# A new order of steps in the ramp and the first quarter of stage 1, in a one-core adaLN, linear attention and gMLP kernel

## The chip, the core and the metric

The kernel runs on one core of a Trainium2 chip. A core has a matrix engine (PE, with its own row PEld for the loading of weights), a vector engine (DVE), an activation engine (ACT), a general engine (POOL) and a queue engine (SP) that here issues most DMAs. Each engine works through its own list of instructions strictly in order and waits at an instruction until its inputs are there and its output buffer is free. The metric is the device time of one execution in microseconds (us).

## What is computed

```
def _A_ref(x, wqkv, w_phi, wo):
    q, k, v = qkv[0], qkv[1], qkv[2]              # of x @ wqkv, 16 heads of 28
    pq = einsum('bhsd,hdf->bhsf', q, w_phi); pk = einsum('bhsd,hdf->bhsf', k, w_phi)
    phi_q = concat([softmax(pq), softmax(-pq)]); phi_k = concat([softmax(pk), softmax(-pk)])
    kv = einsum('bhsf,bhsd->bhfd', phi_k, v); z = sum over s of phi_k
    o = (phi_q @ kv) / (phi_q . z + 1e-6)
    return o @ wo
def _B_ref(x, w_in, w_sp, b_sp, w_out):
    z = gelu(x @ w_in); z1 = z[..., :Fh]; z2 = layernorm(z[..., Fh:])
    g = einsum('ts,bsf->btf', w_sp, z2) + b_sp
    return (z1 * g) @ w_out
mod = silu(c) @ w_mod                              # sa, ca, ga, sb, cb, gb
x = x + ga * _A_ref(layernorm(x) * (1 + ca) + sa, ...)
x = x + gb * _B_ref(layernorm(x) * (1 + cb) + sb, ...)
```

x is 2048 rows of 448, all in bf16; Fh is 896.

## The kernel before

The fast path is written as one long list of words, the table ORDER. Each word is a step; a small loop at the end of `fast_path` runs the words from first to last and so emits the instructions. Since every engine keeps the order in which its instructions were emitted, the table sets the order on each engine and on each DMA queue, and nothing else does. A word reads name:arguments, then `@slot` for a PSUM buffer (A0, A1, A2 of two banks, B0, B1 of one) and `/V`, `/S`, `/G`, `/Y` for the engine that does it (DVE, ACT, POOL, SP). A slot is free again when the step that reads the last result out of it is done.

The 2048 rows are 16 tiles of 128. The steps that matter here:

- `ld:` loads: x0 to x5 are parts of x, wq, wk and wv the three parts of wqkv, phi is w_phi, wsa and wca the shift and scale columns of w_mod for the first half, wsb and wcb for the second, wmga and wmgb the gates.
- Ramp. `FTk`, `FTq` (L795) transpose the key and query weights on PE, 8 transposes a step, `ETk`, `ETq` copy them out (L799 on ACT, L801 on DVE), `bd` (L739) spreads phi into a block-diagonal BD, `PFk`, `PFq` (L811, 4 matmuls) multiply, so that phi is folded into the weights Wk and Wq; `EPk`, `EPq` copy out. `csA`, `ccA` (L747, 16 small matmuls) give shift and scale columns, `esA` and `ecA` copy them (ecA gives the gain column f_ca, L751). `SHk`, `SHq`, `SHv` (L761) work out a shift row, `SCk`, `SCq`, `SCv` (L770 on ACT, L772 on POOL, L774 on DVE) scale the weights by the gain, step 0 out of PSUM, steps 1 to 3 in SBUF. `du` (L712) multiplies zeros, as filler on PE.
- Layer norm of tile i: `l1s` (L818, L819: statistics, on DVE), `l1e`, `l1r` (L822, L823, L826: on POOL for one to four tiles), `l1a` (L829: normalise, on DVE or POOL). Tiles 0 to 3 are turned on PE (`X`, L842) and copied (`XE`), the others by DMA transposes on SP (`T1`, L834).
- Stage 1, per tile: `kM`, `vM` (L852, L860: 4 matmuls), `kE`, `kF` (L855: the two exponentials, on ACT), `vC` (L863: copy, on ACT), `kS` (L866: sums, on DVE), `kR` (L870: reciprocal, on DVE, into one of two buffers), `kP` (L873: f_phik, the normalised features, on DVE or POOL, in a ring of four), `kA` (L883: 8 matmuls that add to kvacc in slot A0). `qM` (L907) and `qE`, `qF` (L912) make query features; `gr`, `ge` (L918, L921) a gate row, `wos`, `wts` (L924) multiply output weights by it. `W:0,u` (L1051) are transposing loads of w_sp on SP.

Stage 2 (`nM` and on) forms the attention output, the second layer norm and the first matmuls of the second half; stage 3 (`gM`, `oM`) mixes over rows and writes out.

Of the kernel before, what the change touches and what calls it, by code (L numbers as in the profile page):

```python
# [486 lines left out]
SHk@B0 XE:3/S XE:2/S ld:wv/Y ld:x3/Y SCk:0/S ld:x4/Y SHv@B1 SCk:2/V SCk:1/V SCv:2/V SCv:3/V l1s:4 l1s:5 l1s:6 l1s:7 l1s:8 l1s:9 l1s:10 ld:wmgb/Y
ld:x5/Y ld:wo/Y ld:wmga/Y SCv:1/S SCv:0/S l1e:4,8/G l1r:4,8 l1a:5/G l1a:4/G SCk:3/S qM:0@A2 vM:0@B0 qF:0 vC:0 qE:0 kM:0@B1 vM:1@A1 vC:1 kE:0 kM:1@B0
vM:2@A2 vM:3@A1 l1a:6/G l1a:7/G kF:0 kF:1 kE:1 vC:2 kM:2@B1 kM:3@B0 kS:0 l1s:11 kS:1 kR:0 l1e:8,12/G l1r:8,12 kP:0/V kR:1 kP:1/G l1a:9/G vC:3 kE:2
qM:1@A2 gr:1@A1 kF:3 kE:3 kF:2 ge:1 qE:1 T1:4,6 kA:0@A0 gr:0@B0 kM:4@B1 qF:1 kF:4 kE:4 kS:2 kS:3 kR:2 l1s:12 T1:6,8 ld:wout/Y qM:2@A1 kA:1@A0 kM:5@B1  # L490
kR:3 kP:2/V l1a:8/G kP:3/G kS:4 l1s:13 kR:4 kP:4/V T1:8,10 W:0,2 W:0,5 l1a:10/G wts:4/G l1a:11/G T1:10,12 ge:0 ld:wsb/S qF:2 kA:2@A0 vM:4@B0 kA:3@A0
kE:5 kF:5 kM:6@B1 l1s:14 l1s:15 l1e:12,16/G l1r:12,16 l1a:13/G vC:4 qE:2 kE:6 kF:6 kA:4@A0 vM:5@B0 kM:7@A2 kM:8@B1 vM:6@A1 kE:7 vC:5 kF:7 kS:5 kR:5
l1a:15/G l1a:14/G kP:5/V kS:6 kS:7 kR:6 kR:7 kP:6/V kP:7/V l1a:12/G T1:12,14 wos:0/G kF:8 T1:14,16 ld:win1/Y W:0,0 W:0,1 ld:wcb/Y W:0,7 ld:bsp/Y W:0,4
vC:6 kA:5@A0 vM:7@B0 kM:9@A2 vM:8@A1 kE:8 kF:9 vC:7 kE:9 kA:6@A0 kM:10@B1 kE:10 kF:10 vC:8 kA:7@A0 kM:11@B0 vM:9@A2 kM:12@B1 kF:11 kE:11 W:0,3
ld:win0/Y vC:9 kS:8 kR:8 kS:9 kR:9 kP:8/G kS:10 kS:11 kR:10 kP:9/G kR:11 kP:10/V kP:11/G kA:8@A0 kE:12 kF:12 vM:10@B0 kM:13@A2 vC:10 kA:9@A0 kF:13
kE:13 kS:12 kR:12 kP:12/G kS:13 kR:13 kP:13/G vM:11@B0 vC:11 kA:10@A0 kM:14@B1 kE:14 kF:14 wts:0/G wos:1/G wts:6/G wos:2/G wts:2/G wts:1/G wos:3/G
kA:11@A0 kS:14 kR:14 kP:14/V vM:12@B0 kM:15@A2 vC:12 kF:15 kE:15 vM:13@B1 vC:13 kA:12@A0 kS:15 kR:15 kP:15/V vM:14@B0 kA:13@A0 vM:15@B1 vC:14 vC:15
kA:14@A0 csB@B0 kA:15@A0 esB KV:0/V KV:1/V KZ:0 KZ:1 qM:3@A2 ccB@B0 nM:0@A1 nM:1@A0 ecB qF:3 nX:0 SHw:3@B0 SHw:2@B1 nX:1 nC:0 nC:1 nS:0 nT:0 nA:0/V
T2:0,1 W:0,6 nT:1 SCw:3,1/G SCw:1,1/G SCw:0,2/V SCw:0,3/V SCw:2,1/V nA:1/G T2:1,2 qE:3 qM:4@A2 qM:5@A1 qF:4 qE:4 nM:2@A0 nM:3@A2 nX:2 nC:2 nX:3 nC:3
nS:1 qF:5 nT:2 nT:3 qE:5 wN:0@B0 wR:0/S SHw:1@B1 nM:4@A1 nM:5@A0 SCw:0,1/S nX:4 nX:5 nC:4 nC:5 nS:2 nA:2/G nT:4 nA:3/G nT:5 nA:4/G wN:1@B0 wQ:0/S  # L500
wR:1/S wQ:1/S SHw:0@B1 SCw:2,0/S l2R:0,2/G l2r:0,2 l2a:0/G SCw:0,0/V nA:5/V T2:2,4 T2:4,6 qM:6@A2 nM:6@A1 nM:7@A0 wN:2@B0 wN:3@B1 qE:6 nX:6 nC:6 nX:7
nC:7 nS:3 nT:6 nT:7 qF:6 wR:2/S wQ:2/S wR:3/S wQ:3/V l2R:2,4/V nA:6/G nA:7/G l2r:2,4 l2a:3/G l2a:2/G qM:7@A2 nM:8@A1 nM:9@A0 wN:4@B0 wM:5@B1 W:1,1
# [12 lines left out]
zN:12/V zN:13/G zQ:14/V yM:3,6@B1 yM:0,3@A1 yM:1,6@B0 yG:0,3 yG:1,6 yM:1,0@A0 yG:1,0 yG:3,6 yM:3,3@A1 yM:0,5@B0 yG:0,5 yG:3,3 yG:0,6 zR:14,16/V
zW:14,16 zN:14/G zN:15/V gM:0,6@B1 gM:0,3@B0 gG:0,3 gM:0,4@A2 gG:0,6 gM:0,2@B0 yM:2,4@B1 yM:2,6@A1 yG:2,6 yG:2,4 gG:0,4 gG:0,2 yM:3,5@A2 yM:3,1@B0
yM:2,3@B1 yG:3,5 wts:5/V yG:2,3 yG:3,1 gM:0,0@A2 gG:0,0 gM:0,5@B0 gG:0,5 yM:2,0@B1 gM:0,1@A2 gG:0,1 gM:1,4@B0 oM:0,0,7@A2 oM:3,0,7@A1 yM:3,4@A0 gG:1,4
oE:0 oM:2,0,7@B0 yM:3,2@A2 yG:3,4 yG:2,0 yG:3,2 guard@A0 gM:1,5@B1 oM:1,0,7@A2 oE:1 oE:2 oE:3 gM:1,2@A0 gG:1,2 gM:1,1@B0 gM:1,3@A2 gM:1,0@A1 gG:1,3
gG:1,0 gM:1,6@A2 oD:0/Y oD:3/Y oD:2/Y gG:1,1 gG:1,5 gG:1,6 gM:2,0@B0 yM:2,2@B1 yG:2,2 W:3,0 W:3,3 W:3,7 W:3,1 W:3,6 W:3,4 W:3,2 gM:2,2@A2 gG:2,0
oM:6,0,7@B0 gM:2,3@B1 oM:4,0,7@A1 gM:2,5@A0 oE:4 gG:2,5 gG:2,3 gM:2,6@A1 gG:2,6 gG:2,2 oM:5,0,7@B1 oE:5 oE:6 gM:2,4@A0 gM:2,1@B0 gG:2,1 oM:7,0,7@B1  # L520
oE:7 W:3,5 oD:1/Y gM:3,3@A2 read gG:2,4 oM:8,0,7@B0 oE:8 oM:10,0,7@B1 oM:9,0,7@B0 oE:9 oE:10 oD:8/Y oD:10/Y oD:6/Y oD:5/Y gM:3,2@A1 gM:3,5@B0
gM:3,1@B1 gG:3,1 gG:3,2 gM:3,6@A0 gM:3,4@B1 gG:3,6 gG:3,4 gG:3,3 gG:3,5 oD:7/Y gM:3,0@A1 oM:11,0,7@B1 gM:4,2@B0 oD:4/Y gG:3,0 oM:12,0,7@A2 oE:11 oE:12
oM:13,0,7@B1 oE:13 gG:4,2 oD:9/Y gM:4,6@A2 gM:4,4@A1 gM:4,3@B0 gM:4,0@B1 gG:4,4 gG:4,3 gG:4,0 gM:4,1@A1 gM:4,5@B0 hint oM:14,0,7@B1 gG:4,1 gG:4,6
gG:4,5 oM:15,0,6@B0 oM:15,6,7@B0 oE:14 oE:15 oD:12/Y oD:13/Y oD:14/Y oD:11/Y oD:15/Y
"""


def fast_path(tc, A_x, A_wqkv, A_w_phi, A_wo, B_w_in, B_w_sp, B_b_sp, B_w_out, c, w_mod, out, flag):
    nc = tc.nc
    S = A_x.shape[1]  # L530
# [82 lines left out]
    scb = aph.tile([DC, KC, P], BF, name="f_scb")  # L613
# [92 lines left out]
            for h in range(2):  # L706
                nc.tensor.matmul(wps[:, h, 0:256], lhsT=zero[64 * h:64 * h + 64, 0:P], rhs=zero[64 * h:64 * h + 64, 0:256], start=True, stop=True)

    def du(n, slot):
        wps = bank(slot, "warm_ps")  # L710
        for _ in range(n):
            nc.tensor.matmul(wps[:, 0, 0:256], lhsT=zero[:, 0:P], rhs=zero[:, 0:256], start=True, stop=True)  # L712
# [465 lines left out]
```

## Time and profile before

| what | us |
|---|---|
| median of 3 runs | 262.6 (262.52 to 263.1) |
| the profiled execution, its own time | 262.55 |
| its span, first instruction to last | 260.8 |
| PE, DVE, ACT, POOL busy | 251.9, 159.1, 107.6, 89.1 |

The span is what the trace shows; the rest of the execution's own time lies around it. In the rows of the timeline the columns are the start (us from the span's start), the time to the end of the last of the instructions that a row merges, engine, line, operation, output and inputs, and in brackets how long the engine stood idle before it and what released it. Matmuls are pipelined: a matmul's row is longer than the step from one matmul's start to the next, so starts are compared with starts.

### The profile page before, as it was taken

How to read it: one execution, taken by the hardware profiler on the slowest of the kernel's cores; microseconds unless marked ns; L12 is line 12 of the kernel's file. 1: busy time of each engine (PE TensorE's matmuls, PEld its weight loads, DVE VectorE, ACT ScalarE, POOL GpSimd, SP SyncE). 2: the span in 40 equal slices, each digit the busy share in tenths (PEclk: the TensorE clock that was granted, in tenths of full speed). 3: DMA queues.
4: the chain of work that ended last, by engine and by line, in shares of the span. 5: the costliest groups of instructions: out<-in, count | busy, mean ns of one | idle time of the engine just before them, and what ended most of it. 6: DMA issues, size and time to landing. Idle time of an engine off the chain costs nothing.

```text
span 260.8 us, 4339 instructions
## 1 busy us (share of the span) xinstructions
PE 251.9 (97%) x1636; PEld 134.8 (52%) x1636; DVE 159.1 (61%) x359; ACT 107.6 (41%) x222; POOL 89.1 (34%) x149
## 2 busy tenths in 40 slices
...
GB/s 170 282 302 124 211 132 224 234 219 64 57 112 134 86 145 114 184 130 176 139 0 3 1 0 0 20 3 75 0 3 161 141 0 0 20 106 0 3 38 62
DMA packets 68655, 25.23 MB, mean 97 GB/s; under 512 B 58129, under 2 KB 68498, under 8 KB 68626
## 3 DMA queue, kind: packets, MB, share of 16 engines
...
q8 instruction: 15, 0.25, 0.4%
q14 instruction: 14, 0.11, 0.1%
...
## 4 chain that ended last, share of the span: by engine, by line
PE 81%; DVE 12%; DMA 2%; ACT 1%; issue 1%; POOL 1%; SPq 0%; ACTq 0%; DVEq 0%
PE g_ps L1059 37%; PE z_ps L1043 9%; PE z_ps L1015 9%; PE o_ps L1072 8%; DVE f_t L955 3%; PE v_ps L860 3%; PE x_ps L971 3%; PE k_ps L852 3%; PE kvacc L883 2%; PE q_ps L907 2%; DMA f_wk_raw<-in_A_wqkv_dram 2%; DVE f_ksum L866 2%; PE num L935 1%; DVE f_phik L873 1%; PE sh_ps L761 1%
## 5 line engine op out<-in xcount | busy, mean ns | idle before, releaser
L1059 PEld LDWEIGHTS <-f_z2n 128*128 128x128 bf16 x560 | 50.1, 98 | 47.0
L1065 DVE TENSOR_TENSOR f_gb<-g_ps,f_bsp 128x512 f32<-128x512 f32 (+2 forms) x35 | 20.4, 583 | 55.8 <-PE g_ps L1059 55.7
L1059 PE MATMUL g_ps<-f_Eq,f_z2n 128*128 128x512 bf16 x224 | 49.5, 379 | 0.0
L1046 ACT ACTIVATE f_z1T<-z_ps 128x512 bf16<-128x512 f32 x28 | 15.6, 592 | 61.8 <-PE z_ps L1043 61.7
L1015 PE MATMUL z_ps<-f_win,f_hT 112*128 112x448 bf16 (+1 forms) x128 | 26.2, 352 | 0.0
L1043 PE MATMUL z_ps<-f_hT,f_win 113*128 113x512 bf16 (+1 forms) x112 | 26.1, 379 | 0.0
L1059 PE MATMUL g_ps<-f_hT,f_z2n 128*128 128x384 bf16 (+1 forms) x224 | 25.1, 272 | 0.0
L1059 PE MATMUL g_ps<-f_wsp,f_z2n 128*128 128x512 bf16 x112 | 24.7, 379 | 0.0
L1072 PE MATMUL o_ps<-f_wout,f_z1T 128*128 128x448 bf16 x112 | 23.0, 352 | 0.0
L1075 DVE TENSOR_TENSOR f_xpad<-o_ps,f_x 128x448 bf16<-128x448 f32 x16 | 9.6, 620 | 20.7 <-PE o_ps L1072 20.7
L1066 DVE TENSOR_TENSOR f_z1T<-f_gb,f_z1T 128x512 bf16<-128x512 f32 (+2 forms) x35 | 20.5, 585 | 1.5
L1015 PEld LDWEIGHTS <-f_hT 112*128 112x128 bf16 (+1 forms) x128 | 12.2, 97 | 12.4 <-DMA f_hT<-f_xpad 0.8
L912 ACT ACTIVATE f_Eq<-q_ps 112x1024 bf16<-112x1024 f32 x16 | 16.1, 1028 | 5.8 <-PE q_ps L907 5.8
L855 ACT ACTIVATE f_E<-k_ps 128x448 bf16<-128x448 f32 x32 | 15.9, 550 | 4.4 <-PE k_ps L852 2.5
L1043 PEld LDWEIGHTS <-f_win 113*128 113x128 bf16 (+1 forms) x112 | 10.9, 97 | 13.1 <-issue 0.2
L866 DVE TENSOR_REDUCE f_ksum<-f_E 128x32 f32<-128x896 bf16 x16 | 16.7, 1060 | 0.7 <-ACT f_E L855 0.7
L955 DVE TENSOR_TENSOR f_t<-num,f_w 128x896 bf16<-128x896 f32 x16 | 16.8, 1084 | 0.4
L1019 ACT ACTIVATE f_z2g<-z_ps 128x896 bf16<-128x896 f32 x16 | 14.7, 917 | 4.0 <-PE z_ps L1015 3.6
L1072 PEld LDWEIGHTS <-f_z1T 128*128 128x128 bf16 x112 | 10.9, 98 | 10.1
L907 PE MATMUL q_ps<-f_hT,f_Wq 113*128 113x512 bf16 (+1 forms) x64 | 15.2, 379 | 0.6 <-DVE f_t L955 0.6
L860 PE MATMUL v_ps<-f_wv,f_hT 113*128 113x448 bf16 (+1 forms) x64 | 14.6, 352 | 0.0
L852 PE MATMUL k_ps<-f_Wk,f_hT 113*128 113x448 bf16 (+1 forms) x64 | 14.4, 352 | 0.0
...
## 6 DMA issues: line engine op xcount, KB each, us to landing
...
```

Source lines behind the costliest of these rows:

```text
L852: nc.tensor.matmul(t[:, 0, 0:D], lhsT=hT[0:KR[m], i, m, :], rhs=Wk[0:KR[m], m, :], start=(m == 0), stop=(m == KC - 1))
L860: nc.tensor.matmul(t[:, 0, 0:D], lhsT=hT[0:KR[m], i, m, :], rhs=wv[0:KR[m], m, :], start=(m == 0), stop=(m == KC - 1))
L866: nc.vector.tensor_reduce(out=ksum[:, i], in_=Er[i % NR][:].rearrange("p s (c f h) -> p (s c) h f", c=4, h=HP), axis=AX.X, op=ALU.add)
L907: nc.tensor.matmul(t[:, u, :], lhsT=Wq[0:KR[m], m, cc * CB:cc * CB + P], rhs=hT[0:KR[m], 4 * st:4 * st + 4, m, :], start=(m == 0), stop=(m ...
L912: nc.scalar.activation(out=Eq[st // 2][0:CB, 2 * c2:2 * c2 + 2, s, (st % 2) * 512:(st % 2 + 1) * 512], in_=ps["q" + str(n)][0:CB, :, :], f ...
L955: nc.vector.tensor_tensor(out=tr[i % 2][:], in0=numv(i)[:, :, :, 0:DH], in1=wr[i // 2 % 2][:, i % 2].unsqueeze(3).to_broadcast([P, 2, H, D ...
L1015: nc.tensor.matmul(t[:, hf, 0:D], lhsT=hT[0:KR[m], i, m, :], rhs=win_s[0:KR[m], m, FH + hf * D:FH + (hf + 1) * D], start=(m == 0), stop=(m ...
L1043: nc.tensor.matmul(t[:, 0, :], lhsT=win_s[0:KR[m], m, fc * P:(fc + 1) * P], rhs=hT[0:KR[m], 4 * st:4 * st + 4, m, :], start=(m == 0), stop ...
L1059: nc.tensor.matmul(g[:, 0, 0:b - a], lhsT=later["z2n"][:, s_, fc * P:(fc + 1) * P], rhs=wspT[t][:, s_, a:b], start=(s_ == 0), stop=(s_ == ...
L1065: nc.vector.tensor_tensor(out=gb, in0=ps["G%d_%d" % (ch, fc)][:, 0, 0:b - a], in1=bsp[:, t * TCHF + a:t * TCHF + b], op=ALU.add)
L1066: nc.vector.tensor_tensor(out=z, in0=gb, in1=z, op=ALU.mult)
L1072: nc.tensor.matmul(ps["o" + str(t)][:, 0, 0:D], lhsT=later["z1T"][:, fc, t * P:(t + 1) * P], rhs=wout_s[:, fc, :], start=(fc == 0), stop=( ...
```

## The change

The words of ORDER up to `vC:6` (tile 6 of stage 1) are put in another order; behind it the words stay in their order and only some slots get other names. The set of steps is the same. Assignments to engines change too: BD goes from DVE to POOL, ETk:0, ETq:0, SCk:0, SCv:0, l1a:0, 4, 11 and 13, wts:4 and kP:3 to DVE, kP:5 and kP:7 and two SCv to POOL, and others between DVE and ACT. `du` takes a second argument that it does not use, and wsb is loaded from SP's queue instead of ACT's.

```diff
-m3 m4 m1/G m2b/V m2a/V ld:x0/Y ld:wq/Y l1s:0 ld:c/S du:3@A2 ct@B0 tbl ce:1 ce:2 l1e:0,1/G l1r:0,1 l1a:0/G ce:3 ce:4 du:11@A2 FTq:0@B1 du:1@A2 FTq:1@B0
-ETq:0/S X:0@A2 XE:0/S ld:wk/Y FTk:1@A1 ETk:1/S FTk:0@B1 ETk:0/S ld:phi/Y ETq:1/V bd/V scb ld:x1/Y l1s:1 l1e:1,2/G l1r:1,2 l1a:1/G PFq:3@B0 PFq:2@A2
...
+m3 m4 m1/G m2b/V m2a/V ld:x0/Y ld:wk/Y ld:phi/Y ld:c/S du:3,0@A2 ct@B0 tbl ce:1 ce:2 l1s:0 du:11,1@A2 FTk:1@B1 ld:wq/Y FTk:0@A0 ld:x1/Y du:1,4@A1
+du:4,3@A1 ETk:0/V bd/G ETk:1/S PFk:1@A1 ld:wsa/Y PFk:2@A2 PFk:0@B1 EPk:1/S FTq:0@A0 l1e:0,1/G ld:x2/Y FTq:1@A1 ld:wca/Y l1r:0,1 EPk:2/S EPk:0/S ce:3
...
-    def du(n, slot):
+    def du(n, k, slot):
```

SP's queue at the start, before and then as changed. f_wk_raw, f_wq_raw and f_wv are the key, query and value weights, f_wm the shift and scale columns:

```order
 L641 DMA f_x<-in_A_x_dram 128x448
-L630 DMA f_wq_raw<-in_A_wqkv_dram 112x4x448
 L630 DMA f_wk_raw<-in_A_wqkv_dram 112x4x448
 L634 DMA f_phi<-in_A_w_phi_dram 112x4x28
+L630 DMA f_wq_raw<-in_A_wqkv_dram 112x4x448
 L642 DMA f_x<-in_A_x_dram 128x448
+L637 DMA f_wm_123<-in_w_mod_dram 112x4x464
 L643 DMA f_x<-in_A_x_dram 128x2x448
```

The key weights and phi are now ahead of the query weights, and the first columns of w_mod ahead of rows 2 and 3 of x.

POOL's list in the first half of stage 1, where f_phik is kP, f_xpad is l1a and f_wo, f_wout are wos and wts. Before:

```order
L873 TENSOR_TENSOR f_phik<-f_E_128,f_kr_134 128x896
L829 TENSOR_SCALAR f_xpad<-f_x,f_nm_147,f_rs_146 128x4x112 x2
L873 TENSOR_TENSOR f_phik<-f_E_130,f_kr_134 128x896
L829 TENSOR_SCALAR f_xpad<-f_x,f_nm_147,f_rs_146 128x4x112
L924 TENSOR_TENSOR f_wout<-f_wout,f_g_rep 128x448
```

and now:

```order
L924 TENSOR_TENSOR f_wo<-f_wo,f_g_rep 112x448
L873 TENSOR_TENSOR f_phik<-f_E_128,f_kr_134 128x896
L822 TENSOR_SCALAR f_rs_146<-f_mv_145 128x4
L823 TENSOR_SCALAR f_nm_147<-f_mv_145 128x4
L826 TENSOR_TENSOR f_rs_146<-f_rs_146,f_mhalf 128x4
L829 TENSOR_SCALAR f_xpad<-f_x,f_nm_147,f_rs_146 128x4x112 x3
```

The gate row of f_wo (wos:0) now stands ahead of the first kP on POOL (kP:1), and the last three of POOL's tiles are normalised (f_rs, f_nm, f_xpad) between it and the next two, kP:5 and kP:7.

DVE's list from kS:4 to kP:6, as changed (f_kr_133 and f_kr_134 are the two buffers of kR):

```order
L870 RECIPROCAL f_kr_134<-f_ksum 128x32
L873 TENSOR_TENSOR f_phik<-f_E_130,f_kr_134 128x896
L829 TENSOR_SCALAR f_xpad<-f_x,f_nm_147,f_rs_146 128x4x112
L870 RECIPROCAL f_kr_133<-f_ksum 128x32
L866 TENSOR_REDUCE f_ksum<-f_E_128 128x32
...
L873 TENSOR_TENSOR f_phik<-f_E_127,f_kr_133 128x896
L866 TENSOR_REDUCE f_ksum<-f_E_130 128x32
L866 TENSOR_REDUCE f_ksum<-f_E_129 128x32
...
L924 TENSOR_TENSOR f_wout<-f_wout,f_g_rep 128x448
L873 TENSOR_TENSOR f_phik<-f_E_129,f_kr_133 128x896
```

kP:3 (first f_phik row), two l1a and wts:4 are new on DVE there, and kP:5 and kP:7 have left it for POOL.

More of the change, by code (lines that the diff above doesn't have):

```diff
@@ L482 @@
 ORDER = """
-m3 m4 m1/G m2b/V m2a/V ld:x0/Y ld:wq/Y l1s:0 ld:c/S du:3@A2 ct@B0 tbl ce:1 ce:2 l1e:0,1/G l1r:0,1 l1a:0/G ce:3 ce:4 du:11@A2 FTq:0@B1 du:1@A2 FTq:1@B0
-ETq:0/S X:0@A2 XE:0/S ld:wk/Y FTk:1@A1 ETk:1/S FTk:0@B1 ETk:0/S ld:phi/Y ETq:1/V bd/V scb ld:x1/Y l1s:1 l1e:1,2/G l1r:1,2 l1a:1/G PFq:3@B0 PFq:2@A2
-PFq:1@A1 EPq:2/S EPq:1/S ld:x2/Y EPq:3/V l1s:2 l1s:3 l1e:2,4/G l1r:2,4 du:4@A0 PFk:0@B0 PFk:2@B1 PFq:0@A2 PFk:1@A0 ld:wsa/Y du:1@A1 csA@A1 EPk:0/S
-EPk:1/S PFk:3@B0 X:1@A0 EPk:3/S XE:1/S EPk:2/S EPq:0/V esA SHq@A2 ld:wca/Y ccA@B0 l1a:3/V X:3@A1 l1a:2/V ecA SCq:0/V SCq:3/V SCq:2/V SCq:1/V X:2@A0
@@ L487 @@
[L487 to L502, printed above, removed]
@@ L515 @@
[L515 to L522, printed above, removed]
```

52 lines of the change are left out of this document (39 added, 13 removed).

## The prediction

> **What bounds the kernel now.** I read the page first, then the work of each engine by stages, then the order in time of the first 60 us.
>
> ```profile
> span 260.8 us, 4339 instructions
> PE 251.9 (97%) x1636; PEld 134.8 (52%) x1636; DVE 159.1 (61%) x359; ACT 107.6 (41%) x222; POOL 89.1 (34%) x149
> 25.00:35.00 10.00, 10.00 (x81) 5.94 (x79) 9.18 (x20) 8.78 (x15) 9.02 (x10) 1.00 1.10 206
> 35.00:45.00 10.00, 9.52 (x73) 5.14 (x71) 9.92 (x15) 7.62 (x17) 7.51 (x7) 1.00 0.75 165
> 45.00:55.00 10.00, 10.00 (x107) 6.65 (x106) 8.61 (x14) 5.50 (x11) 9.83 (x7) 1.00 1.24 229
> ```
>
> The columns of the last three are the stretch, its length, then busy time of PE, PEld, DVE, ACT, POOL. PE never rests long; the clock column (1.00) is full in each. The change adds no work to PE, so it can win or lose only PE's waits up to about 43 us; behind that the two orders of steps are the same. In the first 10 us the loads of weights that stand ahead of the matmuls show the waits:
>
> ```profile
> 5.36 0.49 PEld L795 LDWEIGHTS <-f_wq_raw 112*112 112x112 bf16 x8 [0.82 <-DMA f_wq_raw<-in_A_wqkv_dram]
> 6.87 0.90 PEld L795 LDWEIGHTS <-f_wk_raw 112*112 112x112 bf16 x16 [0.31 <-DMA f_wk_raw<-in_A_wqkv_dram]
> 8.48 0.23 PEld L811 LDWEIGHTS <-f_wTq 112*112 112x112 bf16 x3 [0.19 <-issue]
> 9.29 0.49 PEld L811 LDWEIGHTS <-f_wTk 112*112 112x112 bf16 x8 [0.29 <-ACT f_wTk L799]
> 10.49 0.45 PEld L747 LDWEIGHTS <-f_wm 112*128 112x128 bf16 x15 [0.23 <-issue]
> ```
>
> Behind the first landing (5.36) they add up to 0.31 + 0.19 + 0.29 + 0.23 = 1.0 us. From 10.5 on PE is closed until three short stops late in the first half of stage 1:
>
> ```profile
> 37.39 0.92 PE L860 MATMUL v_ps<-f_wv,f_hT 113*128 113x448 bf16 x4
> 38.40 0.59 PE L883 MATMUL kvacc<-f_vaug,f_phik 128*128 128x116 bf16 x8
> 38.83 0.92 PE L852 MATMUL k_ps<-f_Wk,f_hT 113*128 113x448 bf16 x4
> 39.77 0.59 PE L883 MATMUL kvacc<-f_vaug,f_phik 128*128 128x116 bf16 x8
> 41.72 0.92 PE L852 MATMUL k_ps<-f_Wk,f_hT 113*128 113x448 bf16 x4
> 43.01 0.59 PE L883 MATMUL kvacc<-f_vaug,f_phik 128*128 128x116 bf16 x8 [0.37 <-POOL f_phik L873]
> ```
>
> A group of four v_ps or k_ps matmuls takes 0.76 from start to start (between the rows where nothing waits), a kvacc group 0.43. So PE was ready for tile 6's kvacc (kA:6) at 38.15 and got it at 38.40; kA:8 came 0.53 late at 43.01. These hang on the normalisation kP, on DVE and POOL:
>
> ```profile
> 34.30 0.62 DVE L873 TENSOR_TENSOR f_phik<-f_E,f_kr 128x896 bf16<-128x896 bf16 x1
> 34.84 2.07 DVE L866 TENSOR_REDUCE f_ksum<-f_E 128x32 f32<-128x896 bf16 x2
> 36.83 0.56 DVE L870 RECIPROCAL f_kr<-f_ksum 128x32 bf16<-128x32 f32 x2
> 37.30 2.41 DVE L873 TENSOR_TENSOR f_phik<-f_E,f_kr 128x896 bf16<-128x896 bf16 x2
> 39.64 1.07 DVE L866 TENSOR_REDUCE f_ksum<-f_E 128x32 f32<-128x896 bf16 x1
> 37.84 1.40 POOL L924 TENSOR_TENSOR f_wo<-f_wo,f_g_rep 112x448 bf16<-112x448 bf16 x1
> 54.11 1.03 POOL L924 TENSOR_TENSOR f_wo<-f_wo,f_g_rep 112x448 bf16<-112x448 bf16 x1
> 41.27 3.34 POOL L873 TENSOR_TENSOR f_phik<-f_E,f_kr 128x896 bf16<-128x896 bf16 x2 [2.03 <-ACT f_vaug L863]
> ```
>
> The first row is kP:4 at 0.54 to its successor. The fourth is kP:6 and kP:7, 2.41 instead of 2 x 0.54: they lost 1.3 us, 0.65 each, while POOL worked on the same kind of operation (wos:0, itself 1.40 instead of 1.03). So one such operation on DVE beside one on POOL is not free.
>
> **The change, part by part.**
>
> *Ramp on PE.* The number of steps, fillers (20 matmuls of zeros) and matmuls stays, so PE's arrival at kA:6 is 38.15 plus the new waits less the old 1.0. Durations of the new chain come from these rows and the ones above:
>
> ```profile
> 6.02 0.91 ACT L799 COPY f_wTq<-tps 112x896 bf16<-112x896 bf16 x1 [3.16 <-PE tps L795]
> 6.54 0.62 DVE L801 COPY f_wTq<-tps 112x896 bf16<-112x896 bf16 x1 [2.15 <-PE tps L795]
> 7.08 0.61 DVE L739 TENSOR_TENSOR f_BD<-f_phi,f_bmask 112x448 bf16<-112x448 bf16 x1
> 8.68 0.60 PE L712 MATMUL warm_ps<-f_zero 128*128 128x256 bf16 x4
> 11.78 0.70 DVE L829 TENSOR_SCALAR f_xpad<-f_x,f_nm,f_rs 128x448 bf16<-128x448 bf16 x2 [0.54 <-POOL f_rs L826]
> 12.10 0.54 PE L747 MATMUL cf_ps<-f_scol,f_wm 112*128 112x1 bf16 x16
> 12.68 0.16 DVE L751 TENSOR_SCALAR f_ca<-cf_ps 112x4 f32<-112x4 f32 x1 [0.19 <-PE cf_ps L747]
> 12.88 0.68 DVE L774 TENSOR_SCALAR f_Wq<-sh_ps,f_ca 113x448 bf16<-113x448 f32 x1
> 13.47 0.82 DVE L774 TENSOR_SCALAR f_Wq<-f_Wq,f_ca 112x448 bf16<-112x448 bf16 x3
> 15.19 0.62 DVE L818 BATCH_NORM_STATS2 f_st<-f_x 128x6 f32<-128x448 bf16 x1
> 15.95 0.59 DVE L818 BATCH_NORM_STATS2 f_st<-f_x 128x6 f32<-128x448 bf16 x1
> ```
>
> The key weights take the place of the query weights on the queue, so they land for 5.36. Sixteen transposes at 0.052 each and a first one (0.04 more) run to 6.23, five fillers at 0.11 to 6.77. The second copy (ETk:0) starts on DVE as far behind its transposes as ETq:1 did, 0.6, so at 6.43, and ends at 7.05: wait 0.3. Three PFk (0.67), the query transposes (0.83), PFk:3, a filler, X:0 and csA reach 9.55; ETq:1 ends at 9.6: wait 0.1. Four PFq, SHk (0.76), X:1, ccA (0.40) and SHq end at about 12.7. The gain column ca1 is ready at 12.47 (0.6 behind the start of ccA, as 12.10 to 12.68, and 0.2 more), the four scalings of Wk on DVE and ACT feed kM:0's matmuls one by one: wait 0.35. SHv waits 0.1 for SCq:0. Then qM:1 needs SCq:1, which stands on DVE behind four statistics (0.76 each, 15.19 to 15.95), two scalings out of PSUM (0.60 each, 12.88 to 13.47) and l1a:3: it is done at 18.2 where PE is ready at 17.6: wait 0.6. Sum 0.3 + 0.1 + 0.35 + 0.1 + 0.6 = 1.5. PE reaches kA:6 at 38.15 + 1.5 - 1.0 = 38.65. Bounds: 37.9, if the DVE order costs nothing behind ccA, and 39.3: the wca load has the same bytes ahead of it as before, so it has landed by 12.10 at the latest, where I want it at 11.52.
>
> *BD moves to POOL.* DVE had it at 0.61; POOL's nearest row is 1.03. Before, DVE could start it at 7.08, 0.2 behind the first use of the key weights (6.87), so phi lands by about 5.6 now and BD ends by 6.7, under ETk:0; with that cover gone it would cost PE up to 0.5.
>
> *DVE's list up to kP:6.* From 12.5 on nothing it needs is late, so I add: 12 statistics x 0.75 = 9.0; kS:0 to 7, 8 x 0.99 = 7.9 (34.84 to 36.83 is two); 8 reciprocals x 0.25 = 2.0; kP:0, 2, 3, 4, 6 at 0.54 = 2.7; four l1a at 0.35 = 1.4; three PSUM scalings 1.8; four others at 0.25 = 1.0; wts:4, new here, 0.54. Sum 26.3, so kP:6 would end at 38.8, if POOL never stands in its way. kA:6 then starts at 38.8 and kA:8 at 0.43 + 0.76 + 0.43 + 3 x 0.76 = 3.9 later: 42.7, which is 0.3 **before** 43.01. kP:8 on POOL (1.7) ends inside that.
>
> *Where POOL stands in its way.* POOL's list now has wos:0 and kP:1 close to kP:2, kP:5 close to kP:4, and kP:7, released by kR:7, just ahead of wts:4 and kP:6. Before, POOL's long kP ran beside reductions only (39.64 shows one at 1.07, not stretched). The price of one meeting is 0 to 1.7 (the whole POOL operation, half of 3.34); nearest is 0.65. I take 0.65 for kP:2, 0.65 for the pair wts:4 and kP:6, and 0.3 for kP:4, since kP:5 and kP:4 get ready within 0.3 us and either may be first: 1.6 us. kP:6 ends at 40.4, PE waits 1.75 there, kA:8 starts at 44.3, **+1.3 us**. From 45 to 55 PE has no gap that could give it back.
>
> The page "SBUF — State Buffer" of the Trainium skill, section "Who interferes with whom", says that a DVE operation with two SBUF inputs and a GpSimd operation that reads SBUF exclude each other: who issues first holds the pair of ports for the whole instruction, and a reduction never contends. The rows at 37.30 and 39.64 agree.
>
> *SP's queue.* The wsb load leaves ACT and stands between two transposes that feed hT:
>
> ```profile
> 27.10 0.35 ACTq L637 DMA_DIRECT2D f_wm<-in_w_mod_dram  x1
> 45.89 0.53 SPq L637 DMA_DIRECT2D f_wm<-in_w_mod_dram  x1
> 29.79 3.92 SPq L1051 DMA_TRANSPOSE f_wsp<-in_B_w_sp_dram  x2
> 33.81 6.70 SPq L834 DMA_TRANSPOSE f_hT<-f_xpad  x3
> ```
>
> It costs SP 0.53 ahead of T1:12,14 and gives ACT 0.35, which had waits there. Three wsp pieces now precede T1:10,12 instead of two; at 2 us each from about 28.3 (by the sum of POOL's list up to l1a:8) it is issued at 34.2 and, at 3.5 to 5 us, landed by 39.2, when kM:10 asks at 39.3 or later. Cost 0, up to 0.5 if kP:6 is not late.
>
> **Sum.** 262.55 us was the profiled execution (span 260.8 and 1.75 around it), within 0.1 of the median 262.6. -0.3 + 1.6 = +1.3 gives 263.9 us.
>
> **Rivals.**
> 1. No meeting on DVE and POOL costs anything. For it: 34.30 (kP:4) ran at 0.62 with POOL busy on other steps. Against: 37.30. Then kA:8 is 0.3 early, 262.3; if the 0.6 wait on SCq:1 also falls away, DVE's list starts to lead by as much and it is 261.7. It decides from the point where kP:6 ends before 38.6.
> 2. The full lock. kP:4 loses the whole of kP:5 and the pair wts:4/kP:6 the whole of kP:7, 1.7 each, with 0.65 for kP:2: 4.05 - 0.3 = +3.75, 266.3. For it: each stands right behind an operation that releases the POOL one. Against: POOL waits too when DVE is first (1.40 for wos:0). The rule of the Trainium skill's page "SBUF — State Buffer" gives this price wherever POOL's operation is issued first.
> 3. The change doesn't do what it says: the new waits in the ramp equal the old and the stops at 38 to 43 stay as they were, 262.6. For it: PE's total is the same and both lists are dense; against: DVE's list is different throughout.
>
> **How the numbers follow.** Forecast 0.47, rival 1 0.33 (0.25 of it beyond what a measurement tells from no change, 0.2% or 0.5 us, and 0.08 within), rival 2 0.10, rival 3 0.10. So faster 0.25, same 0.18, slower 0.57. The forecast's own range, with one meeting more or less and the ramp's bounds, is 262.8 to 265.2; with rivals it reaches from 261.8 to 265.6.
>
> **What would show it.** First transposes at 5.4 and first PFk at 7.1; kM:0 near 13 with a short wait ahead of it; a wait of qM:1 near 17.6 on f_Wq from DVE; kP:6 on DVE ending near 40.4 with kP rows of 1 to 2 us beside POOL's kP; kA:8 near 44.3. It is wrong if PE reaches kA:8 before 43.0, if all kP rows on DVE stay at 0.6, or if PE stops for hT or a DMA instead.

## The result, and the profile after

| | before | after |
|---|---|---|
| median of the runs that stand side by side | 263.0 us | 270.0 us |
| ratio, with its 95% interval | | 1.025 (1.021 to 1.029) |
| profiled execution, its span | 262.55, 260.8 us | 269.96, 268.2 us |

The change made the kernel 7.0 us slower; the forecast was 1.3 us slower, and 270.0 lies outside its range. Four of the six executions took 270.0 to 270.3 us and two 268.1 and 268.2, with a higher granted clock in these two; the second experiment tells why. A ratio is estimated over all executions that stand side by side and need not be the quotient of the medians: 1.025 is 6.5 us. Of the runs further down, e3 has two executions at 270.3 us with a granted clock near 0.98, which are in neither its median nor its ratio.

Where the time went is in PE's waits. This view of the kernel after lists, for all of the span, who PE waited for, the sum, how often, and the longest (its first five rows):

```profile
PE kvacc L883 <- DVE f_phik L873: 3.3, 3, 2.2
PE warm_ps L712 <- DVE f_zero L670: 1.2, 1, 1.2
PE kvacc L883 <- ACT f_E L855: 0.9, 1, 0.9
PE q_ps L907 <- DVE f_Wq L774: 0.6, 1, 0.6
PE z_ps L1015 <- DMA f_hT<-f_xpad: 0.4, 1, 0.4
```

The second row is the start of the program, in both kernels. The first is new: PE waits for DVE's kP. PE's rows around the longest stop, in order of time (start, length, engine, step, how many):

```profile
40.41 1.00 PE L883 MATMUL kvacc<-f_vaug,f_phik 128*128 128x116 bf16 x16 [0.77 <-DVE f_phik L873]
41.26 0.92 PE L852 MATMUL k_ps<-f_Wk,f_hT 113*128 113x448 bf16 x4
42.02 0.93 PE L860 MATMUL v_ps<-f_wv,f_hT 113*128 113x448 bf16 x4
45.14 0.95 PE L883 MATMUL kvacc<-f_vaug,f_phik 128*128 128x116 bf16 x8 [2.20 <-DVE f_phik L873]
45.89 1.70 PE L852 MATMUL k_ps<-f_Wk,f_hT 113*128 113x448 bf16 x4
...
50.46 0.58 PE L883 MATMUL kvacc<-f_vaug,f_phik 128*128 128x116 bf16 x8
```

The row at 45.14 is kA:6, the last one kA:8. Before, kA:8 started at 43.01, so it is 7.45 us late, and the span grew by 7.4: all of the loss lies ahead of kA:8, and nothing behind gives any back. Two things are to be seen. PE stops for 2.20 us for kP:6. And behind that stop its matmuls are slow: the four at 45.89 take 1.70 where the four at 41.26 take 0.92, so from kA:6 to kA:8 it needs 5.3 us, where the forecast had 3.9. DVE's kP rows, and what POOL did at the time:

```profile
29.00 2.56 DVE L873 TENSOR_TENSOR f_phik<-f_E,f_kr 128x896 bf16<-128x896 bf16 x1
38.26 2.10 DVE L873 TENSOR_TENSOR f_phik<-f_E,f_kr 128x896 bf16<-128x896 bf16 x1
42.99 2.10 DVE L873 TENSOR_TENSOR f_phik<-f_E,f_kr 128x896 bf16<-128x896 bf16 x1
28.40 1.04 POOL L924 TENSOR_TENSOR f_wo<-f_wo,f_g_rep 112x448 bf16<-112x448 bf16 x1
29.38 1.70 POOL L873 TENSOR_TENSOR f_phik<-f_E,f_kr 128x896 bf16<-128x896 bf16 x1
38.18 1.70 POOL L873 TENSOR_TENSOR f_phik<-f_E,f_kr 128x896 bf16<-128x896 bf16 x1
42.78 1.83 POOL L873 TENSOR_TENSOR f_phik<-f_E,f_kr 128x896 bf16<-128x896 bf16 x1 [2.90 <-DVE f_kr L870]
```

These are kP:2, kP:4 and kP:6 on DVE, which take some 0.6 alone, and wos:0, kP:1, kP:5 and kP:7 on POOL. Each time POOL was first, by 0.08 us at 38.2, and each time DVE ended 0.47 to 0.48 us behind POOL's end (31.56 behind 31.08, 40.36 behind 39.88, 45.08 behind 44.61). An operation that ends the same 0.48 us behind POOL's, whether it took 2.56 or 2.10, did not run slowly beside POOL's; it ran when POOL's was over. And kP:2 waited for two of them: it was there at 29.00, wos:0 ended at 29.44, yet kP:1, queued right behind it, went first.

### The profile page after: what moved, and what is told of

Same layout as the page of the kernel before. It is cut to its first block, busy times and chain, and to the rows that moved or that the text cites. A ratio compares the mean times of both kernels' runs of the same rounds, so it can differ in the third digit from the quotient of the medians.

```text
span 268.2 us, 4335 instructions
## 1 busy us (share of the span) xinstructions
PE 254.4 (95%) x1627; PEld 136.4 (51%) x1636; DVE 163.2 (61%) x361; ACT 105.8 (39%) x220; POOL 89.1 (33%) x149
## 4 chain that ended last, share of the span: by engine, by line
PE 77%; DVE 16%; DMA 3%; issue 1%; ACT 0%; SPq 0%; DVEq 0%
PE g_ps L1059 36%; PE z_ps L1043 9%; PE z_ps L1015 9%; PE o_ps L1072 8%; DVE f_phik L873 4%; PE k_ps L852 3%; DVE f_ksum L866 3%; PE x_ps L971 3%; DVE f_st L818 2%; DVE f_t L955 2%; PE q_ps L907 2%; PE kvacc L883 2%; PE v_ps L860 2%; DMA f_wk_raw<-in_A_wqkv_dram 2%; DMA f_hT<-f_xpad 1%
## 5 line engine op out<-in xcount | busy, mean ns | idle before, releaser
L1015 PE MATMUL z_ps<-f_win,f_hT 112*128 112x448 bf16 (+1 forms) x128 | 26.2, 352 | 0.5 <-DMA f_hT<-f_xpad 0.4
L1015 PEld LDWEIGHTS <-f_hT 112*128 112x128 bf16 (+1 forms) x128 | 12.2, 97 | 13.1 <-DMA f_hT<-f_xpad 1.8
L873 POOL TENSOR_TENSOR f_phik<-f_E,f_kr 128x896 bf16<-128x896 bf16 x8 | 13.8, 1736 | 6.9 <-DVE f_kr L870 4.9
L852 PE MATMUL k_ps<-f_Wk,f_hT 113*128 113x448 bf16 (+1 forms) x64 | 15.5, 366 | 0.3 <-DVE f_Wk L774 0.3
L907 PE MATMUL q_ps<-f_hT,f_Wq 113*128 113x512 bf16 (+1 forms) x64 | 15.2, 379 | 0.6 <-DVE f_Wq L774 0.6
```

Of the source, the lines that this page charges most:

```text
L852: nc.tensor.matmul(t[:, 0, 0:D], lhsT=hT[0:KR[m], i, m, :], rhs=Wk[0:KR[m], m, :], start=(m == 0), stop=(m == KC - 1))
L873: eng.tensor_tensor(out=pr[i % NR][:, 0:2 * D].rearrange("p (a f h) -> p a f h", a=8, h=HP), in0=Er[i % NR][:].rearrange("p s (c f h) -> p ...
L907: nc.tensor.matmul(t[:, u, :], lhsT=Wq[0:KR[m], m, cc * CB:cc * CB + P], rhs=hT[0:KR[m], 4 * st:4 * st + 4, m, :], start=(m == 0), stop=(m ...
L1015: nc.tensor.matmul(t[:, hf, 0:D], lhsT=hT[0:KR[m], i, m, :], rhs=win_s[0:KR[m], m, FH + hf * D:FH + (hf + 1) * D], start=(m == 0), stop=(m ...
```

## The experiments

All but e3, e4, e7, e8, e9 and e12 are edits of the kernel after. Each ratio is to the kernel before, run beside it (its medians there: 262.6 for e1 to e4, 263.1 for e5 to e8, 262.9 for e9 to e11, 263.7 for e12). Each profile is of one execution. By the trace's record of the granted clock, PE came to full clock at 11.4, 11.0 and 10.5 us in those of e5, e10 and e12, and at 4.5 to 7.7 us in the others; all that follows in these three stands 1.5 to 2 us late, so their times are read against each other within one profile.

| run | what | median us | ratio (95%) |
|---|---|---|---|
| e1_apart | kP:2, kP:4, kP:6, wts:4 moved | 268.1 | 1.022 (1.018 to 1.027) |
| e2_fill | fillers in the stop ahead of kA:6 | 268.4 | 1.022 (1.018 to 1.025) |
| e3_newramp | new ramp, old rest | 265.4 (of four) | 1.011 (1.008 to 1.014) |
| e4_newrest | old ramp, new rest | 269.2 | 1.022 (1.015 to 1.028) |
| e5_kp2 | kP:2's meeting removed | 267.5 | 1.016 (1.012 to 1.020) |
| e6_nomeet | all three meetings removed | 265.8 | 1.011 (1.007 to 1.015) |
| e7_oldramp | old ramp, rest of e6 | 264.7 | 1.008 (1.005 to 1.011) |
| e8_wosaway | before, wos:0 moved | 262.5 | 0.998 (0.995 to 1.001) |
| e9_oldscale | e7, SCk:3 earlier | 264.7 | 1.007 (1.004 to 1.010) |
| e10_scq | e6, SCq:1 earlier | 265.9 | 1.010 (1.007 to 1.013) |
| e11_scq_kf | e10, kF:6 later | 264.9 | 1.007 (1.004 to 1.010) |
| e12_wosaway5 | e8 again | 262.8 | 0.997 (0.995 to 0.999) |

### e1_apart: kP moved out of POOL's way

```diff
- kS:2 kR:2 l1e:8,12/G l1s:15 l1r:8,12 ... l1a:9/G kP:2/V
+ kS:2 kR:2 l1e:8,12/G kP:2/V l1s:15 l1r:8,12 ... l1a:9/G
- kF:7 kR:4 vM:6@B1 ... T1:12,14 kP:4/V kS:7 kP:5/G kS:6 kR:7 vM:7@A1 kR:6 wts:4/V ... kP:6/V
+ kF:7 kR:4 kP:4/V vM:6@B1 ... T1:12,14 kP:5/G kS:7 kS:6 kR:6 kP:6/V kR:7 vM:7@A1 ...
- kP:1/G kE:5
+ kP:1/G wts:4/G kE:5
```

> The changed kernel with DVE's list altered at three places, so that no kP of DVE stands beside a kP of POOL: kP:2 ahead of l1s:15, kP:4 directly behind kR:4, and kS:7, kS:6, kR:6, kP:6 ahead of kR:7 (which releases kP:7 on POOL); wts:4 back on POOL behind kP:1. Theory A (DVE and POOL exclude each other; the three kP that took 2.56, 2.09 and 2.10 us instead of 0.57 delay kA:6, and the stop of PE that follows costs some clock): the three kP fall to 0.6 to 0.9, kA:6 starts near 40 instead of 45.1, the clock row stays at 1.00 and the time is 262.5 to 264.5. Theory B (the new loads and the ramp cost it): DVE's kP get short but PE stops elsewhere, the time stays above 267.

Measured: 268.1, a miss for theory A, and in the range of theory B, though not for its reason. kP:4 and kP:6 fell to 0.63 and 0.62 and PE's long stop went, but kP:2 became worse, as DVE's and POOL's rows of this run show:

```profile
28.77 3.13 DVE L873 TENSOR_TENSOR f_phik<-f_E,f_kr 128x896 bf16<-128x896 bf16 x1
28.75 1.03 POOL L924 TENSOR_TENSOR f_wo<-f_wo,f_g_rep 112x448 bf16<-112x448 bf16 x1
29.74 1.69 POOL L873 TENSOR_TENSOR f_phik<-f_E,f_kr 128x896 bf16<-128x896 bf16 x1
```

wos:0 was first by 0.02 us (and a normalisation of POOL ran ahead of it until 28.78), and again kP:1 behind it went ahead of DVE: kP:2 ended at 31.90, 0.48 behind kP:1. So the move made one of the three meetings longer, and how much the three cost together was open until e5 and e6.

### e2_fill: the clock behind the stop

```diff
- kE:9 kA:6@A0 kM:10@B0
+ kE:9 du:20,0@B0 kA:6@A0 kM:10@B0
```

> The changed kernel with 20 more matmuls of zeros on PE (2.2 us) ahead of kA:6, inside its stop of 3.1 us, and nothing else. Theory A1 (the stop lets the clock of PE fall, 0.68 in the stretch 45 to 50, and this costs 1.4 to 1.8 us on top of the stop): kA:6 stays at 45.1, the clock stays at 1.00, kvacc and k_ps groups behind it take 0.43 and 0.76 again, and the time falls from 270.0 to about 268.2 in every execution. Rival (the stop alone costs all of it and the two levels of 268.2 and 270 have another cause): the time stays at 269.5 to 270.3.

Measured: 268.4, as theory A1 had it, and its four executions lie within 267.9 to 268.6, where the kernel after had two groups. The stretches of 10 us (start and end, length, busy time of PE, PEld, DVE, ACT, POOL, then the granted clock) of the kernel after:

```profile
35.00:45.00 10.00, 6.90 (x63) 4.04 (x60) 9.93 (x15) 5.59 (x11) 6.60 (x6) 0.99 0.98 186
45.00:55.00 10.00, 9.86 (x77) 6.37 (x78) 8.47 (x14) 5.84 (x12) 6.39 (x4) 0.84 1.31 226
```

and with the fillers:

```profile
35.00:45.00 10.00, 8.96 (x81) 5.87 (x78) 9.93 (x16) 5.59 (x11) 6.47 (x6) 1.00 0.91 186
45.00:55.00 10.00, 9.99 (x89) 6.35 (x89) 8.83 (x14) 7.07 (x15) 7.82 (x5) 1.00 1.17 228
```

kA:6 starts at about the same time in both (45.02 here), but the clock is 1.00 instead of 0.84, and PE gets 89 matmuls done instead of 77. Shorter stretches of the kernel after show the clock at half from 44.8 to 48.1 and full again from 48.2:

```profile
44.80:48.10 3.30, 2.96 (x20) 2.07 (x21) 2.93 (x5) 0.42 (x1) 1.47 (x1) 0.50 1.08 233
48.20:55.00 6.80, 6.80 (x59) 4.19 (x58) 5.74 (x9) 5.31 (x12) 4.83 (x4) 1.00 1.42 222
```

With matmuls of zeros, which compute nothing, kA:8 starts at 48.91 instead of 50.46:

```profile
45.02 0.59 PE L883 MATMUL kvacc<-f_vaug,f_phik 128*128 128x116 bf16 x8
...
48.91 0.58 PE L883 MATMUL kvacc<-f_vaug,f_phik 128*128 128x116 bf16 x8
```

From kA:6 to kA:8 that is 3.89 us instead of 5.32: the stop costs its own length (2.20 us; the 3.1 of the expectation counts from the start of the group ahead of it) and then 1.4 us by the clock. The medians differ by 1.6 us, the ratios by 0.3% or 0.8 us with intervals that overlap, as not every execution of the kernel after lost it. The two near 268.2 have a mean granted clock of 0.998 and 1.000 over the whole execution, like the four of e2 (0.998 to 1.000); the four at 270.0 and above have 0.991 to 0.993. The Trainium skill's page "TensorE: Matmul & The Clock Gate", Part 1, has the clock halved after an idle window of about 3.4 us; here a stop of 2.20, with 0.77 some 4 us ahead of it, was enough in four executions of six.

### e3_newramp and e4_newrest: the two halves apart

The table is split at the end of the ramp (all steps to the last SC and the first four tiles' normalisation, and the loads up to wo): e3 has the new words in front and the old behind, e4 the other way round.

> The ramp as changed (loads, PE, DVE, ACT and POOL up to the scaled weights and tiles 0 to 3 in hT), with all later steps in the order and on the engines of before. Theory A (the order of kP in stage 1 costs it): the ramp's share is its own waits, some 0.5 to 1.0 us, so 263.0 to 264.5. Theory B (the ramp costs it): above 267.

> The ramp as before, with all later steps in the changed order and on the changed engines. Theory A: kP:2, kP:4 and kP:6 on DVE still meet POOL's operations and take 1.5 to 2.6 us, the time is 266 to 270. Theory B: it is at 262.5 to 264.

Measured: 265.4 and 269.2. The rest carries most, as its theory had it, with 3.2 us of waits for f_phik where the whole change has 3.3; e4 also waits 0.9 us for f_Wk and 0.7 for the load of f_wmg, which neither parent does. The ramp costs 1.1% too, more than theory A had and less than theory B. In the profile of e3, an execution of 270.3 us, PE has a stop of its own, 1.4 us for f_xpad at 13.9 to 15.2, which neither parent has, and the clock stood at half for 10 us behind it:

```profile
15.00:20.00 5.00, 4.00 (x16) 1.67 (x17) 2.57 (x8) 1.71 (x4) 1.25 (x2) 0.51 1.13 247
20.00:25.00 5.00, 5.00 (x14) 1.93 (x13) 4.23 (x13) 2.19 (x3) 2.46 (x5) 0.50 0.42 94
```

That the other executions of e3 have this stop too, without the loss of clock, is not shown; if they have, part of the 1.1% is the mixture's own.

### e5_kp2 and e6_nomeet: one meeting removed, and all three

```diff
- l1a:9/G kP:2/V T1:4,6
+ l1a:9/G T1:4,6
- kS:3 wos:0/G vC:3 ... kE:4 l1s:14 kF:6
+ kS:3 vC:3 ... kE:4 l1s:14 kP:2/V kF:6
- nA:1/G T2:1,2
+ nA:1/G wos:0/G T2:1,2
```

e5 is the kernel after with these; e6 is e1 with them, and with wts:4 next to wos:0.

> The changed kernel with kP:2 moved two places down DVE's list (behind l1s:14) and POOL's wos:0 moved far down (behind nA:1), so that kP:2 meets neither wos:0 nor kP:1. kP:4 and kP:6 still start beside kP:5 and kP:7. Theory A (DVE's list is the bound and each meeting adds what POOL's operation has left): kP:2 takes 0.6 instead of 2.56 us, everything behind it on DVE is 2.0 us earlier, kP:4 and kP:6 still take about 2.1, time 268.0 (267.2 to 268.8) against 270.0. Theory B (the kP:2 meeting is hidden, because PE waits for ACT's f_E at kA:0 anyway): 269.5 to 270.3.

> e1_apart with the same two moves, and wts:4 moved behind nA:1 too: none of the three kP beside a POOL operation. Theory A: the 2.5 us that kP:2 lost in e1_apart are gone, kP:6 ends near 40.7, kA:8 starts near 45.6, time 265.6 (264.8 to 266.4), which leaves 3 us for the ramp. Theory B (behind the meetings lies a second bound, POOL's or ACT's list, that holds kA:8 where it is): 267.3 to 268.3.

Measured: e5 267.5, e6 265.8, both as theory A had them. In e5 DVE's kP:2, kP:4 and kP:6, then POOL's kP:5 and kP:7:

```profile
32.67 0.59 DVE L873 TENSOR_TENSOR f_phik<-f_E,f_kr 128x896 bf16<-128x896 bf16 x1
...
38.77 0.62 DVE L873 TENSOR_TENSOR f_phik<-f_E,f_kr 128x896 bf16<-128x896 bf16 x1
42.01 2.10 DVE L873 TENSOR_TENSOR f_phik<-f_E,f_kr 128x896 bf16<-128x896 bf16 x1
38.81 2.12 POOL L873 TENSOR_TENSOR f_phik<-f_E,f_kr 128x896 bf16<-128x896 bf16 x1 [0.48 <-DVE f_kr L870]
41.80 1.83 POOL L873 TENSOR_TENSOR f_phik<-f_E,f_kr 128x896 bf16<-128x896 bf16 x1 [0.87 <-PE kvacc L883]
```

This is the rule in one run. At 38.8 DVE was first, by 0.04 us, and took 0.62 while POOL's kP:5 took 2.12 instead of 1.69; at 41.8 POOL was first, and DVE took 2.10. So the expectation that kP:4 would stay at 2.1 was wrong, by the luck of 0.04 us, and e5 has two meetings less, not one. Who starts first holds the other for the whole operation, as the Trainium skill's page "SBUF — State Buffer", section "Who interferes with whom", states it; the runs agree in each meeting of two such operations but kP:2's, where kP:1 started behind DVE's and went ahead.

What kP:6's meeting costs alone, e5 doesn't show. In its profile kA:8 starts at 48.05, 2.4 us later than in e6, but kM:0 starts at 16.08 there and at 14.05 in e6, so 2.0 us of it are the ramp's; and the intervals of the two ratios overlap.

In e6 none of the three meets a kP or a gate row of POOL (kP:4 waits 0.1 us for a normalisation). kP:6 and PE's kA:6, kA:7 and kA:8:

```profile
40.14 0.63 DVE L873 TENSOR_TENSOR f_phik<-f_E,f_kr 128x896 bf16<-128x896 bf16 x1
41.31 0.58 PE L883 MATMUL kvacc<-f_vaug,f_phik 128*128 128x116 bf16 x8
...
42.94 0.59 PE L883 MATMUL kvacc<-f_vaug,f_phik 128*128 128x116 bf16 x8 [0.29 <-POOL f_phik L873]
...
45.65 0.53 PE L883 MATMUL kvacc<-f_vaug,f_phik 128*128 128x116 bf16 x7
```

kP:6 ends at 40.77 (45.08 after), PE no longer waits for it, and kA:8 stands 2.6 us behind 43.01, most of what is left of the loss. So the meetings, with the clock that they pulled down, cost 4.8 us at kA:8 in the profiled executions (50.46 less 45.65), and 3.6 us by the ratios (1.025 less 1.011); 1.1%, some 2.7 us by the medians, are not theirs. Not all of this is the change's either: e6 has a stop of its own in stage 2, for the wos:0 that it moved,

```profile
67.03 0.92 PE L971 MATMUL x_ps<-f_wo,f_oT 112*128 112x448 bf16 x4 [1.13 <-POOL f_wo L924]
```

and from kA:8 to the end of the span it needs 218.3 us, where the kernels before and after need 217.7.

### e7_oldramp and e9_oldscale: the rest without meetings behind the old ramp

e7 is the old ramp with the rest of e6; e9 removes a wait that only this mixture has:

```diff
- SCv:1/S SCv:0/S SCk:3/S
+ SCk:3/S SCv:1/S SCv:0/S
```

> The ramp of the kernel before (everything up to the last SC, with its loads) and behind it the rest of e6_nomeet. Theory A (meetings and ramp are all that the change costs): 262.3 to 264.0, kP:6 ends between 38.8 and 39.7. Theory B (the new order of the query, value and key work behind the ramp has a cost of its own): 264.5 to 266.5.

> e7_oldramp with one word moved: the last scaling of the key weights (SCk:3, on ACT) ahead of two value scalings, since PE waited 0.9 us for it there, a wait that neither kernel has. Theory A: that wait goes and the time falls by as much, to 263.8 (263.3 to 264.3); the new order behind the ramp then costs less than 1 us when no kP stands beside a POOL operation. Theory B: PE stops later instead (for DVE's list or a DMA): 264.4 to 265.0.

Measured: 264.7 for both, misses for theory A and in the range of theory B. The wait of 0.9 us for SCk:3 went in e9 and nothing was won; PE stopped later instead. Its waits in e9 between 14 and 46 us:

```profile
21.84 0.93 PE L918 MATMUL gr_ps<-f_wmg,f_scb 112*128 112x448 bf16 x4 [0.57 <-DMA f_wmg<-in_w_mod_dram]
31.98 0.58 PE L883 MATMUL kvacc<-f_vaug,f_phik 128*128 128x116 bf16 x8 [0.41 <-ACT f_E L855]
41.70 0.59 PE L883 MATMUL kvacc<-f_vaug,f_phik 128*128 128x116 bf16 x8 [0.29 <-POOL f_phik L873]
```

Together 1.27 us, against 0.37 + 0.09 in the same stretch before. The first, for a load, is again one that neither kernel has, and from kA:8 to the end e9 needs 218.5 us, 0.8 more than before, with the same stop of 1.1 us for wos:0 as e6. So of the 0.7% (0.4 to 1.0%), some 1.8 us, that the new order behind the ramp seems to cost without a meeting, up to 1.4 us can be the experiment's own.

### e10_scq and e11_scq_kf: which of the small waits counts

```diff
- SCq:0/V kF:0 SHv@B1 SCv:1/G l1s:5 XE:2/S l1s:7 kF:1 SCv:0/V kE:3 SCq:1/V
+ SCq:0/V SCq:1/V kF:0 SHv@B1 SCv:1/G l1s:5 XE:2/S l1s:7 kF:1 SCv:0/V kE:3
```

is e10, on e6; e11 moves one step more:

```diff
- kF:6 kF:4 kP:1/G kE:5 l1s:12 W:0,5 qM:2@A2 kF:5
+ kF:4 kP:1/G kE:5 l1s:12 W:0,5 qM:2@A2 kF:5 kF:6
```

> e6_nomeet with one word moved: SCq:1 on DVE directly behind SCq:0, ahead of two statistics and a value scaling, so that qM:1 does not wait 0.57 us for it. Theory A (behind the ramp DVE's list sets the time, through kP:2, ACT's kF:6 and kA:0): the wait of qM:1 goes, that of kA:0 on f_E grows from 0.6 to about 1.2, time as e6_nomeet, 265.4 to 266.1. Theory B (PE's own waits in the ramp are the loss): 264.9 to 265.4.

> e10_scq with ACT's kF:6 moved behind kF:5, so that kF:4, kE:5 and kF:5 don't stand behind an exponential that waits for DVE's kP:2. Theory A (kP:2 reaches PE through ACT's queue): ACT's stop of 1.3 us ahead of kF:6 no longer holds kF:5, the wait of kA:0 goes, and 0.5 to 1.2 us come out: 264.5 to 265.2. Theory B (DVE's list holds kA:6 a few us later anyway): 265.4 to 266.1.

Measured: 265.9 and 264.9, both as theory A had them. In e10 the wait of qM:1 is gone, and the one at kA:0, 0.64 in e6, is longer:

```profile
34.98 0.58 PE L883 MATMUL kvacc<-f_vaug,f_phik 128*128 128x116 bf16 x8 [1.52 <-ACT f_E L855]
```

What holds kA:0 is a chain over three engines. kF:6 may write f_E only when kP:2 has read the buffer, and kF:4, kE:5 and kF:5 stand behind it in ACT's list. ACT's row in e6:

```profile
31.34 2.29 ACT L855 ACTIVATE f_E<-k_ps 128x448 bf16<-128x448 f32 x5 [1.33 <-DVE f_phik L873]
```

In e11 that chain is cut, and kA:0 starts with no wait:

```profile
31.86 0.58 PE L883 MATMUL kvacc<-f_vaug,f_phik 128*128 128x116 bf16 x8
```

By the medians one us came out by moving one exponential, by the ratios 0.7 us, with intervals that overlap; the trace shows the wait gone. 0.7% (0.4 to 1.0%) stays, and 0.9 us of it lies behind kA:8 (218.6 us from there to the end), with the stop for wos:0 as in e6.

### e8_wosaway and e12_wosaway5: the same price in the kernel before

```diff
- kP:6/V kP:7/V l1a:12/G T1:12,14 wos:0/G kF:8
+ kP:6/V kP:7/V l1a:12/G T1:12,14 kF:8
- nA:1/G T2:1,2
+ nA:1/G wos:0/G T2:1,2
```

> The kernel before with one word moved: POOL's wos:0, which stands beside DVE's kP:6 and kP:7 there, behind nA:1. Theory A: the two kP take 0.62 us each instead of 2.41 together less what l1a:12 still costs (0.5), DVE's list is 0.7 to 1.2 us ahead from there, and PE, which waited 0.4 us for f_phik, gains at most that: 262.0 to 262.6. Theory B (no price from wos:0): the kP keep their 1.04 and 1.45 us, time as before.

> e8_wosaway once more, with more executions, since its ratio to the kernel before was 0.998 with an interval on both sides of 1. If POOL's wos:0 costs DVE and through it PE's 0.37 us ahead of kA:8, the ratio stays near 0.9985 and the interval closes below 1; if the stop of 0.37 us is hidden, the ratio moves to 1.000.

Measured: e8 262.5, its interval on both sides of 1; e12 262.8 against 263.7, ratio 0.997 (0.995 to 0.999). kP:6 and kP:7, 2.41 together before, are 1.13 in e12:

```profile
38.82 1.13 DVE L873 TENSOR_TENSOR f_phik<-f_E,f_kr 128x896 bf16<-128x896 bf16 x2
```

In e8 they are 1.58, as the second waited there for a normalisation of POOL. This version is 0.3% (0.1 to 0.5%) faster than the kernel before. The profiles don't show where PE wins it: its stop for f_phik ahead of kA:8 is gone, but PE waits for a transposing load just ahead of it instead, here e8's row and then e12's (the slowest of its twelve executions):

```profile
42.05 0.93 PE L852 MATMUL k_ps<-f_Wk,f_hT 113*128 113x448 bf16 x4 [0.26 <-DMA f_hT<-f_xpad]
44.17 0.93 PE L852 MATMUL k_ps<-f_Wk,f_hT 113*128 113x448 bf16 x4 [1.22 <-DMA f_hT<-f_xpad]
```

So the price on DVE is shown by the rows, and the gain of the whole by the ratio of e12 alone.

## Why the prediction was wrong

The sign and the mechanism were right: DVE's kP beside POOL's operations, and PE waiting for kP:6. The size was not, and the 6.1 us between 263.9 and 270.0 come apart as the forecast's own terms do, by the time of kA:8 (forecast 44.3, measured 50.46).

- **Where POOL stands in its way: the term that was mis-sized most.** The forecast took 1.6 us (0.65 + 0.65 + 0.3); kP:6 ended 4.3 us later than in e6 (45.08 and 40.77): +2.7. The 0.65 came from the row of the kernel before in which the two losses, 1.3 us, were shared over two kP. Read against POOL's rows it shows two operations waited for, the last normalisation and all of wos:0 (37.84, 1.40):

```profile
35.06 2.81 POOL L829 TENSOR_SCALAR f_xpad<-f_x,f_nm,f_rs 128x448 bf16<-128x448 bf16 x4
```

  Taken one by one, kP:6 (37.30, 1.04 long) ended 0.47 behind the end of this row, at 37.87, and kP:7 (38.27, 1.45 long) 0.48 behind the end of wos:0, at 39.24. So a kP that finds POOL at work takes what POOL has left and 0.48 more. An estimate by this rule, with 1.7 for kP:5 and kP:7, has 1.5 to 1.6 us of loss each for kP:4 and kP:6, where 0.3 and 0.65 were taken; 1.5 each was measured. The forecast also let DVE be first at kP:4 half the time; it was second by 0.08 us. And it had one meeting at kP:2, where POOL kept two in a row. Rival 2 had this mechanism at 266.3, with the small price for kP:2; it was given 0.10 and was the nearest. The list of e6 up to kP:6 is also shorter by wts:4 and kR:7, some 0.5 us, so the split between this item and the next is no better than that.
- **DVE's list up to kP:6: 2 us short.** Without any meeting the forecast had 38.8, with wts:4 on DVE; e6, without it, has 40.77. The list starts 0.7 us later than assumed (the gain column is ready at 13.2 in e6, where 12.5 was taken), and the round figures were all a little low: by the trace of e6 from start to start the twelve statistics take 9.5, with 0.4 of waiting (9.0 forecast), the eight sums 8.25 (7.9), seven reciprocals 2.3 (eight for 2.0), the small scalings 1.3 (1.0).
- **The clock: in no term.** From kA:6 to kA:8 the forecast counted 3.9 us at full clock; it was 5.3, +1.4, and e2 got that back by filling the stop. With 2.7 and 2.0 that is the 6.1 us.
- **Ramp on PE.** The order and the places of the waits were right, 0.27 ahead of kM:0 (0.35 forecast) and 0.56 ahead of qM:1 on f_Wq from DVE (0.6 forecast), but all of it 1 us later: the first PFk started at 8.09 (7.1 forecast), kM:0 at 14.14 (13). The rows say why:

```profile
5.34 1.74 PE L795 MATMUL tps<-f_ident,f_wk_raw 112*112 112x112 bf16 x16 [0.33 <-DMA f_wk_raw<-in_A_wqkv_dram]
6.87 1.07 PE L712 MATMUL warm_ps<-f_zero 128*128 128x256 bf16 x5
8.09 0.80 PE L811 MATMUL pf_ps<-f_BD,f_wTk 112*112 112x112 bf16 x12
```

  Sixteen transposes in 1.74 are 0.093 apart, not 0.052. By the trace's record of the granted clock, full speed was there at 4.7 us in the profiled execution of the kernel before and at 7.2 here (the clock column of the views shows 1.00 ahead of the record's first entry, so it doesn't show this). That moment varies with either ramp: in e3, with the new one, the sixteen took 1.03, and in e8, e9 and e12, with the old one, the first eight took 1.0 instead of 0.62; it came at 4.9 to 11.4 us in the eight profiles with the new ramp and at 4.5 to 10.5 in the six with the old. Whether the new ramp makes a late one more frequent is not shown. The forecast read one execution's luck as a duration.
- **PE's arrival.** 38.65 was forecast for kA:6; in e6, with nothing of DVE in the way there, it was 41.31. The forecast charged kP:2 to DVE's list alone. Its second way to PE, over ACT's kF:6 to kA:0, was missed; e11 shows it, 0.7 to 1.0 us. This is also why rival 1 (no price for a meeting, 262.3 or 261.7) falls: with no meetings the kernel is still 1.1% slower than before, though part of that is e6's own stop for wos:0.
- **BD on POOL and the load on SP's queue** cost nothing, as said: BD ran on POOL from 5.58 to 6.5, under the transposes of the key weights, and PE waits for no f_hT ahead of kA:8 (the 0.4 us of its list are in stage 2, L1015).
- **The row at 39.64.** It was to show that POOL's long kP doesn't stretch a reduction of DVE, but POOL stood idle there, from 39.24 to 41.27. The reading holds for later rows: two reductions from 42.35 on took 2.01 us beside POOL's kP.

What stays open is how the 2.7 us of e6 divide between ramp and rest. The new ramp with the old rest costs 1.1%, the old ramp with the new rest without meetings 0.7%, and both together no more than 1.1%: the halves don't add, and each mixture has small waits of its own, 0.6 us net for the moved wos:0 in e6 among them.
